# First head of a routed attention kernel: identity in a transfer of its own, first exponential ahead of the next head's copies, codes in another order

## The chip, the cores and the metric

The kernel runs on one core of a Trainium2 chip. A core has five engines with an instruction queue each: PE (TensorE, matrix products; its weight loads are listed as PEld), DVE (VectorE), ACT (ScalarE), POOL (GpSimd) and SP (SyncE, which here only issues transfers). An engine works its queue in order and waits on semaphores that other engines or transfers raise. The metric is the device time of one execution in microseconds (us), the median over several runs.

## The reference

Bucketed attention, then a routed mixture of experts, then a gated product. Only the first part matters here:

```python
q_bits = (np.einsum('bhsd,dk->bhsk', q, proj) > 0)      # 6 bits per query, the same for keys
q_bucket = np.sum(q_bits * powers, axis=-1)
mask = q_bucket[:, :, :, None] == k_bucket[:, :, None, :]
scores = np.where(mask, scale * q @ k^T, -1000000000.0)  # B=2, H=8, S=768, D=64, fp32
attn = exp(scores - max) / (sum + 1e-09)
out = attn @ v
```

A query attends only to the keys of its bucket. The result goes through a router of 8 experts (each token to one of them) and a last product pair; those stages are not touched.

## The kernel before, in words

The 16 pairs of batch and head are called heads 0 to 15. One head has 768 queries, which are 6 tiles of 128; tiles are numbered through all heads by `g`, so head 0 has tiles 0 to 5 and head 1 begins with tile 6.

Inputs of a head come transposed, queries and keys in one buffer `x` (128 partitions, 1536 columns), of which there are two (`xp`, two buffers), so the inputs of head 2 go into the buffer of head 0. For fp32 precision each operand is taken apart: `split_a` (ACT, L105) makes the rounded part `tq` (queries) or `tk` (keys), `split_b` makes the low part `bq` (DVE L117 for the difference, POOL or ACT L118 for a copy) or `bk` (POOL or DVE L120 and L121).

The bucket test is part of the score product. `hash_mm` (PE L130, tile `m`) projects the inputs, and 12 rows of bits, the codes, go into rows 64 to 76 of `tq` and `tk`; with them the product of a query and a key of other buckets comes out far away. For head 0 `hash_code` (DVE L137) writes these rows directly, 384 columns at a time. For all other heads `hash_codes` (DVE L144) writes a tile `code`, and four transfers on SP's queue (L149; two halves of `tq`, then two of `tk`) carry its rows into place. They may start only when the copies that read those rows of `tq` and `tk` are over.

One tile `g` then runs through these steps:

- `scores(g)`: four products on PE (L160 with `tk`, `tq` and the codes; L161 with the low parts), two for each half of the keys, into one of two PSUM buffers `s`
- `smax(g)`: a reduction on DVE (L166, `mm`) and a small operation (L167, `sb`) that gives scale and bias
- `sexp(g)`: the exponential on ACT (L175), into `p`
- `tposes(g)`: six transposes on PE (L188, `tp`) against the identity `ident`, which is the first 128 columns of the constants `cs`; then two copies into `pt` (L192 on ACT, L194 on DVE, by a table)
- later, in the next head, `av_step`: products with V (PE L203)

The order of each engine's queue is that of the code (`tc.manual_schedule()`). In the loop over tiles, the pass of tile `g` first issues `scores(g + 1)` and `smax(g + 1)`, then `set_up(g)` in head 0, then the transposes of tile `g`; `side(pos)` puts exponential, splits and codes before, between or behind the two halves of the transposes, by the table `K`. A few products of a unit matrix (`heat`) run on PE while the first inputs come in. A single element copy `held` on POOL makes POOL wait for the reduction that was issued last.

Of the kernel before, what the change touches and what calls it, by code (L numbers as in the profile page):

```python
# [15 lines left out]
ALU = mybir.AluOpType  # L16
# [5 lines left out]
S, D, NB, NH = 768, 64, 2, 8  # L22
# [12 lines left out]
def attn_moe_kernel(ctx: ExitStack, tc: tile.TileContext, xin, cst, projd, wblk, wmoe, w2in, out):  # L35
    nc = tc.nc
# [69 lines left out]
            T[h, i][:, lo:lo + n], X[h][:, i * S + lo:i * S + lo + n], ACTF.Copy, scale=(-0.125, 1.0)[i]  # L106
        )

    def split_b(h, i, lo=0, n=S):
        copy = POOL.tensor_copy if h or i else ACT.copy  # L110
        x = X[h][:, i * S + lo:i * S + lo + n]
        if lo == 0:
            B[h, i] = tb.tile([128, S], F32R, tag="b" + "qk"[i], name="b" + "qk"[i])
        b = B[h, i][:, lo:lo + n]
        t = T[h, i].bitcast(F32)[:, lo:lo + n]
        if i == 0:
            DVE.scalar_tensor_tensor(out=b[:64], in0=x[:64], scalar=-0.125, in1=t[:64], op0=ALU.mult, op1=ALU.subtract)  # L117
            copy(b[64:], t[64:])  # L118
        else:
            (POOL if h else DVE).tensor_tensor(out=b[64:], in0=x[64:], in1=t[64:], op=ALU.subtract)  # L120
            copy(b[:64], t[:64])  # L121
# [342 lines left out]
    def after(ins, done):  # L464
        ins = ins.ins
        for other in done:
            tc.add_manual_dep(ins, other.name, dep, reason="reads what all the scatters wrote")
# [169 lines left out]
    with tc.manual_schedule():  # L637
# [9 lines left out]
        for j, q in ((2, nc.sync), (3, nc.sync), (0, nc.scalar), (1, nc.sync)):  # L647
            x0_in.append(q.dma_start(out=X[0][:, j * 384:(j + 1) * 384], in_=xin[0, :, j * 384:(j + 1) * 384]).ins)
        nc.scalar.dma_start(out=thr, in_=cst[:, C_THR:C_THR + 2])
        load(1, x0_in)  # L650
        nc.sync.dma_start(out=cs, in_=cst)
        nc.sync.dma_start(out=V[0], in_=xin[0, :, 2 * S:].rearrange("p (k d) -> p k d", d=D))
        nc.sync.dma_start(out=wb, in_=wblk[:, :640 * 2].rearrange("p (h n) -> p h n", h=NH))
        nc.sync.dma_start(out=wl, in_=wblk[:, 640 * 2:])
# [17 lines left out]
        split_a(0, 0, 0, 384)  # L672
        hash_code(0, 2)
        split_b(0, 0, 0, 384)
        hash_code(0, 3)
        hash_code(0, 0)
        scores(0)
        split_a(0, 0, 384, 384)
        split_b(0, 0, 384, 384)
        hash_code(0, 1)  # L680
        smax(0)
        split_a(1, 0)
        split_a(1, 1)
        sexp(0)
        load(2)

        def set_up(k):
            if k == 0:
                split_b(1, 0)
                POOL.tensor_copy(held, pt_[0][:, 0:1])  # L690
            elif k == 1:
                split_b(1, 1)
            elif k == 2:
                POOL.memset(oh, 0.0)
                zero = wraw.tile([128, 512], F32, tag="wr0", name="zero")
                POOL.memset(zero, 0.0)
                zeros.append(zero)
                DVE.tensor_copy(tri, cs[:, C_TRI:C_TRI + 128])
            elif k == 5:
                DVE.tensor_scalar(  # L700
                    out=tokc.bitcast(I32)[:, :, 0], in0=cs[:, C_TOK:C_TOK + 12], scalar1=-float(E * C), scalar2=None,
                    op0=ALU.add,
                )
                DVE.tensor_scalar(
                    out=base2, in0=cs[:, C_BASE:C_BASE + 8], scalar1=1.0 / 128, scalar2=None, op0=ALU.mult
                )
# [32 lines left out]
        qa, qb = (0, 4), (4, 2)  # L739
        for g in range(NG):  # L740
            h, t = divmod(g, NT)
            if t == 1 and h + 3 < NHD:
                load(h + 3)
            if g + 1 < NG:
                scores(g + 1)
                smax(g + 1)
            if g < NT:
                set_up(g)
            if 2 * NT <= g < 2 * NT + (E * C + N) // 256:
                for i in (g - 2 * NT,):  # L750
                    nc.sync.dma_start(
                        out=xr[i * 256:(i + 1) * 256].rearrange("(p r) d -> p r d", p=128),
                        in_=zeros[0].bitcast(U32).unsqueeze(1).to_broadcast([128, 2, 512]),
                    )
            if g == 6 * NT:
                for n in range(4):
                    for part in range(2):
                        w_load(n, part)
            if g == 10 * NT + 1:
                r = router(0)  # L760
                todo = [r["s1"], r["s1b"], None, lambda: (r["s2"](), r["s2c"]()), r["s2b"], r["s4"], r["s4b"]]
                for f in r["sc"]:
                    todo += [f, None]
                todo += [r["s4c"], None, None, None, r["s3a"], None, r["s3b"], None, None, None, r["s5"]]
            early, late = [], []
            if h < L:
                if t == (1 if h else 0):
                    early.append(lambda: hash_mm(h + 1))
                if h:
                    for k in AV_AT.get(t, ()):  # L770
                        early.append(lambda k=k: av_step(h - 1, k))
                if h > 1 and t == 4:
                    (late if K["oul"] else early).append(lambda: o_out(h - 2))
            elif t < 3:
                av_step(h - 1, 2 * t)
                av_step(h - 1, 2 * t + 1)
                if t == 0:
                    o_out(h - 2)
                if t == 2:
                    o_evac(h - 1)  # L780
            elif t == 3:
                o_out(h - 1)
            else:
                k = 3 * (t - 4)
                av_group(h, qa, (k, k + 1, k + 2))
                if t == 5:
                    o_evac(h, qa)
            for f in early:
                f()
            if h and h < L and t == 5 and not K["avl"].count(5):  # L790
                o_evac(h - 1)
            if g > 10 * NT + 1 and todo:
                f = todo.pop(0)
                if f:
                    f()

            def side(pos):
                if g + 1 < NG and K["se" if 0 < h < L else "se0"][t] == pos:
                    sexp(g + 1)
                if h < L and (t, pos) == (1, 0):  # L800
                    hash_codes(h + 1)
                for i in range(2):
                    if h + 2 < NHD and K["sa" if h > 1 else "sa0"][i] == (t, pos):
                        split_a(h + 2, i)
                    if h + 2 < NHD and K["sb" if h > 1 else "sb0"][i] == (t, pos):
                        if t == 5:
                            POOL.tensor_copy(held, last[0])
                        split_b(h + 2, i)

            side(0)  # L810
            tposes(g, 0)
            side(1)
            tposes(g, 1)
            for f in late:
                f()
            if h and h < L and t == 5 and K["avl"].count(5):
                o_evac(h - 1)
            side(2)
            for f in extra.get((h - L + 1, t), ()):
                f()  # L820
        o_out(L, qa)
# [680 lines left out]
```

## Time and profile before

| | |
|---|---|
| median of 3 runs | 722.79 us (722.61 to 722.83) |
| the profiled execution, its own time | 724.47 us |
| its span, first to last instruction | 722.7 us |
| mean granted clock of PE | 0.994 |
| busy: PE, DVE, ACT, POOL | 705.2, 556.8, 448.1, 283.4 us |

The span is what the views of the trace cover; the execution's own time is 1.77 us longer. The profiled execution is one of its own, 1.68 us above the median of the runs without a profile, so a shift is added to either. PE is busy 98% of the span, but matrix products are pipelined and their ends are modelled, so that alone doesn't say that PE sets the pace everywhere. In a row of a timeline the bracket gives the idle time of the engine in front of the instruction and what ended it. PEclk is the clock that PE was granted: 1.00 is 2.4 GHz, 0.50 is 1.2 GHz.

### The profile page before, as it was taken

The numbers are of one execution on the slowest core, as the hardware profiler recorded it, in microseconds if no ns is written. First come the engines' busy times: TensorE is split into PE (matmuls) and PEld (weight loads), VectorE is DVE, ScalarE is ACT, GpSimd is POOL, SyncE is SP. The second block draws the span as 40 slices with busy tenths as digits, with TensorE's granted clock in tenths as the row PEclk, the third lists the DMA queues.
The fourth block names the chain that finished last, engine by engine and source line by source line (L and its number), as shares of the span: only waits on it lengthen the run. The fifth ranks groups of instructions, "written<-read, shape, count | busy, mean of one in ns | idle before, by whom it ended". The sixth has DMA issues, their size and how long they took to land.

```text
span 722.7 us, 13158 instructions
## 1 busy us (share of the span) xinstructions
PE 705.2 (98%) x4505; PEld 604.2 (84%) x4506; DVE 556.8 (77%) x1105; ACT 448.1 (62%) x962; POOL 283.4 (39%) x316
## 2 busy tenths in 40 slices
PE   7899999999999999999999999999999999999995
PEld 6667667667766699999999999999999999999994
DVE  5777887789777778788888878886886877777644
ACT  5787877787877637677778766575444453444320
POOL 4243334322556348845443303333322332223224
PEclk9999999999999999999999999999999999999998
DMA  7348261123212038699899741132121222122013
GB/s 241 107 164 308 85 222 59 59 65 112 104 49 64 15 128 254 174 257 213 237 288 245 229 129 59 40 107 88 59 62 55 88 76 71 55 63 59 0 51 127
DMA packets 53432, 88.01 MB, mean 122 GB/s; under 512 B 19872, under 2 KB 23280, under 8 KB 53360
## 3 DMA queue, kind: packets, MB, share of 16 engines
q1 hardware_dynamic: 50688, 80.61, 37.7%
q0 software_dynamic: 2304, 6.31, 2.3%
q8 instruction: 37, 0.61, 0.3%
q14 instruction: 35, 0.29, 0.1%
q10 hardware_dynamic: 368, 0.20, 0.1%
HBM read 69.65 MB, written 13.12 MB: 115 GB/s over the span
## 4 chain that ended last, share of the span: by engine, by line
PE 84%; issue 4%; DVE 4%; POOL 2%; DMA 2%; ACT 2%; SPq 0%; POOLq 0%; ACTq 0%; DVEq 0%
PE tp L188 9%; PE av L203 8%; PE y L1033 6%; PE s L161 4%; PE s L160 4%; PE h L995 4%; PE h L994 4%; PE h L993 3%; PE aba L1270 3%; PE aba L1272 3%; PE abb L1270 3%; PE aba L1271 3%; PE abb L1272 3%; PE abb L1271 3%; PE y L1034 3%
## 5 line engine op out<-in xcount | busy, mean ns | idle before, releaser
L166 DVE TENSOR_REDUCE mm<-s 128x1 f32<-128x768 f32 x96 | 91.1, 949 | 26.7 <-PE s L161 25.8
L175 ACT ACTIVATE p<-s,sb 128x768 f32<-128x768 f32 x96 | 95.0, 989 | 21.2 <-DVE sb L167 20.4
L188 PEld LDWEIGHTS tp<-cs,p 128*128 128x128 f32 x576 | 64.9, 141 | 37.9 <-ACT p L175 24.4
L188 PE MATMUL tp<-cs,p 128*128 128x128 f32 x576 | 82.7, 280 | 6.4 <-DMA cs<-cst 2.9
L516 DVE TENSOR_TENSOR wl<-wr,wh 128x512 fp32r<-128x512 f32 x125 | 83.2, 705 | 4.9 <-ACT wh L515 1.1
L192 ACT ACTIVATE pt<-tp 128x384 f32<-128x384 f32 x143 | 65.1, 487 | 34.7 <-PE tp L188 34.7
L964 POOL TENSOR_TENSOR pc<-t,pc 128x256 fp32r<-128x256 f32 x38 | 33.1, 873 | 134.8 <-ACT pc L963 119.2
L1033 PE MATMUL y<-hl,wh 128*128 128x448 f32 x224 | 75.0, 378 | 0.6 <-DVE hl L1007 0.5
L515 ACT ACTIVATE wh<-wr 128x512 fp32r<-128x512 f32 x128 | 73.7, 624 | 1.3 <-DMA wr<-wmoe 1.2
L160 PE MATMUL s<-tk,tq 76*128 76x384 f32 x192 | 73.7, 384 | 0.3 <-DVE tq L137 0.3
L994 PE MATMUL h<-xl,wh 128*128 128x224 f32 x256 | 70.3, 275 | 0.5 <-DVE xl L450 0.3
L995 PE MATMUL h<-xh,wl 128*128 128x224 f32 x256 | 70.6, 276 | 0.0
L993 PE MATMUL h<-xh,wh 128*128 128x224 f32 x256 | 70.3, 275 | 0.2 <-ACT xh L449 0.2
L203 PE MATMUL av<-pt,v 128*64 128x384 f32 x360 | 68.0, 499 | 0.2 <-DVE r L238 0.2
L161 PE MATMUL s<-bk,bq 128*128 128x384 f32 x192 | 65.6, 342 | 0.0
L1034 PE MATMUL y<-hl,wl 128*128 128x224 f32 x224 | 59.5, 266 | 0.0
L964 POOL TENSOR_TENSOR pc<-s,pc 128x256 fp32r<-128x256 f32 x44 | 38.0, 875 | 33.0 <-ACT pc L963 32.0
L118 POOL CAST bq<-tq 64x768 fp32r<-64x768 f32 x15 | 21.2, 1414 | 74.8 <-ACT tq L105 47.4
L1160 ACT ACTIVATE gh<-p 128x384 fp32r<-128x384 f32 x21 | 11.0, 526 | 63.2 <-DVE p L1289 63.2
L993 PEld LDWEIGHTS h<-xh,wh 128*128 128x128 f32 x256 | 48.9, 191 | 1.5 <-ACT xh L449 0.4
L994 PEld LDWEIGHTS h<-xl,wh 128*128 128x128 f32 x256 | 49.1, 192 | 1.0 <-DVE xl L450 0.5
L203 PEld LDWEIGHTS av<-pt,v 128*64 128x64 f32 x360 | 21.9, 136 | 32.8 <-issue 24.5
(264 smaller groups left out, 2002.6 us busy)
## 6 DMA issues: line engine op xcount, KB each, us to landing
wr<-wmoe SPq DMA_DIRECT2D x128, 256.0 KB
r<-w2in SPq DMA_DIRECT2D x36, 512.0 KB
x<-xin SPq DMA_DIRECT2D x30, 384.0 KB
xr<-zero SPq DMA_DIRECT2D x13, 512.0 KB
v<-xin SPq DMA_DIRECT2D x16, 192.0 KB
wb<-wblk SPq DMA_DIRECT2D x1, 640.0 KB
x<-xin SPq DMA_DIRECT2D x3, 192.0 KB
tq<-code SPq DMA_DIRECT2D x30, 18.0 KB
```

The costliest lines, as they stand in the source:

```text
L160: PE.matmul(p[:, c, :384], T[h, 0][:76, qs], T[h, 1][:76, sl], start=True, stop=False)
L161: PE.matmul(p[:, c, :384], B[h, 0][:, qs], B[h, 1][:, sl], start=False, stop=True)
L166: DVE.tensor_reduce(out=m[:, 1:2], in_=st[g][:, :, :384], axis=AX.XY, op=ALU.min)
L175: ACT.activation(p.rearrange("p (c n) -> p c n", c=2), st.pop(g)[:, :, :384], ACTF.Exp, scale=scl.pop(g), bias=nbs.pop(g), accum_out=sums[ ...
L188: PE.transpose(ps[:, j * 128:(j + 1) * 128], pt_[g][:, k * 128:(k + 1) * 128], ident)
L203: PE.matmul(av[h][c * 64:(c + 1) * 64, :384], v, PT[h][:, k, c * 384:(c + 1) * 384], start=(k == 0), stop=(k == NT - 1), skip_group_check= ...
L516: eng.tensor_tensor(out=l, in0=r, in1=h.bitcast(F32), op=ALU.subtract)
L993: PE.matmul(ps, wh, xh, start=first, stop=False)
L994: PE.matmul(ps, wh, xl, start=False, stop=False)
L995: PE.matmul(ps, wl, xh, start=False, stop=last)
L1033: PE.matmul(p, wh[:, w], hl, start=(f == 0), stop=False, skip_group_check=True)
L1034: PE.matmul(p[:, 0], wl[:, w], hl[:, 0], start=False, stop=(f == 7), skip_group_check=True)
```

## The change

It touches the first head alone. The identity is transferred by itself when head 0's inputs have landed, ahead of head 1's inputs; the other constants follow where all of them stood. Head 0's codes are written in the order keys' first half, queries' first half, keys' second half; the queries' second half and the low part of that half move behind the reductions of tiles 0 and 1. ACT makes head 1's splits at the ends of tiles 0 and 1, behind the first exponentials, and no longer ahead of them. POOL makes the low part of head 1's keys in two halves, in the passes of tiles 1 and 2, and the low part of head 1's queries follows in the pass of tile 2. The projection of head 1 (`hash_mm(1)`) goes from the pass of tile 0 to that of tile 1, its codes (`hash_codes(1)`) from the pass of tile 1 to that of tile 3, and head 3's inputs (`load(3)`) from tile 1 to tile 4.

```diff
--- before.py
+++ after.py
@@ -106,7 +106,7 @@
             T[h, i][:, lo:lo + n], X[h][:, i * S + lo:i * S + lo + n], ACTF.Copy, scale=(-0.125, 1.0)[i]
         )
 
-    def split_b(h, i, lo=0, n=S):
+    def split_b(h, i, lo=0, n=S, parts=(0, 1)):
         copy = POOL.tensor_copy if h or i else ACT.copy
         x = X[h][:, i * S + lo:i * S + lo + n]
         if lo == 0:
@@ -114,8 +114,12 @@
         b = B[h, i][:, lo:lo + n]
         t = T[h, i].bitcast(F32)[:, lo:lo + n]
         if i == 0:
-            DVE.scalar_tensor_tensor(out=b[:64], in0=x[:64], scalar=-0.125, in1=t[:64], op0=ALU.mult, op1=ALU.subtract)
-            copy(b[64:], t[64:])
+            if 0 in parts:
+                DVE.scalar_tensor_tensor(
+                    out=b[:64], in0=x[:64], scalar=-0.125, in1=t[:64], op0=ALU.mult, op1=ALU.subtract
+                )
+            if 1 in parts:
+                copy(b[64:], t[64:])
         else:
             (POOL if h else DVE).tensor_tensor(out=b[64:], in0=x[64:], in1=t[64:], op=ALU.subtract)
             copy(b[:64], t[:64])
@@ -647,8 +651,9 @@
         for j, q in ((2, nc.sync), (3, nc.sync), (0, nc.scalar), (1, nc.sync)):
             x0_in.append(q.dma_start(out=X[0][:, j * 384:(j + 1) * 384], in_=xin[0, :, j * 384:(j + 1) * 384]).ins)
         nc.scalar.dma_start(out=thr, in_=cst[:, C_THR:C_THR + 2])
+        after(nc.sync.dma_start(out=ident, in_=cst[:, C_ID:C_ID + 128]), x0_in)
         load(1, x0_in)
-        nc.sync.dma_start(out=cs, in_=cst)
+        nc.sync.dma_start(out=cs[:, C_TRI:], in_=cst[:, C_TRI:])
         nc.sync.dma_start(out=V[0], in_=xin[0, :, 2 * S:].rearrange("p (k d) -> p k d", d=D))
         nc.sync.dma_start(out=wb, in_=wblk[:, :640 * 2].rearrange("p (h n) -> p h n", h=NH))
         nc.sync.dma_start(out=wl, in_=wblk[:, 640 * 2:])
@@ -672,25 +677,24 @@
         split_a(0, 0, 0, 384)
         hash_code(0, 2)
         split_b(0, 0, 0, 384)
+        hash_code(0, 0)
         hash_code(0, 3)
-        hash_code(0, 0)
         scores(0)
         split_a(0, 0, 384, 384)
-        split_b(0, 0, 384, 384)
-        hash_code(0, 1)
+        split_b(0, 0, 384, 384, (1,))
         smax(0)
-        split_a(1, 0)
-        split_a(1, 1)
         sexp(0)
         load(2)
 
         def set_up(k):
             if k == 0:
+                split_b(0, 0, 384, 384, (0,))
+                hash_code(0, 1)
+            elif k < 3:
+                POOL.tensor_copy(held, last[0])
+                split_b(1, 1, (k - 1) * 384, 384)
+            if k == 2:
                 split_b(1, 0)
-                POOL.tensor_copy(held, pt_[0][:, 0:1])
-            elif k == 1:
-                split_b(1, 1)
-            elif k == 2:
                 POOL.memset(oh, 0.0)
                 zero = wraw.tile([128, 512], F32, tag="wr0", name="zero")
                 POOL.memset(zero, 0.0)
@@ -739,7 +743,7 @@
         qa, qb = (0, 4), (4, 2)
         for g in range(NG):
             h, t = divmod(g, NT)
-            if t == 1 and h + 3 < NHD:
+            if t == (1 if h else 4) and h + 3 < NHD:
                 load(h + 3)
             if g + 1 < NG:
                 scores(g + 1)
@@ -764,7 +768,7 @@
                 todo += [r["s4c"], None, None, None, r["s3a"], None, r["s3b"], None, None, None, r["s5"]]
             early, late = [], []
             if h < L:
-                if t == (1 if h else 0):
+                if t == 1:
                     early.append(lambda: hash_mm(h + 1))
                 if h:
                     for k in AV_AT.get(t, ()):
@@ -797,7 +801,7 @@
             def side(pos):
                 if g + 1 < NG and K["se" if 0 < h < L else "se0"][t] == pos:
                     sexp(g + 1)
-                if h < L and (t, pos) == (1, 0):
+                if h < L and (t, pos) == ((1, 0) if h else (3, 0)):
                     hash_codes(h + 1)
                 for i in range(2):
                     if h + 2 < NHD and K["sa" if h > 1 else "sa0"][i] == (t, pos):
@@ -816,6 +820,8 @@
             if h and h < L and t == 5 and K["avl"].count(5):
                 o_evac(h - 1)
             side(2)
+            if g < 2:
+                split_a(1, 1 - g)
             for f in extra.get((h - L + 1, t), ()):
                 f()
         o_out(L, qa)
```

Three places show how the order moves; the number in a name tells buffers and tiles apart and is not the same in both kernels. ACT, from the second split of head 0's queries on (`tq`, `tk` of `x_149` are head 1's, `p` is an exponential, `pt` a copy of transposes), before:

```order
L118 CAST bq_247<-tq_244 64x384
L105 ACTIVATE tq_264<-x_149 128x768
L105 ACTIVATE tk_266<-x_149 128x768
L175 ACTIVATE p_268,sums_100<-s_252,sb_261 128x768
L175 ACTIVATE p_293,sums_100<-s_276,sb_281 128x768
L192 ACTIVATE pt_295<-tp_296 128x3x128
L192 ACTIVATE pt_295<-tp_301 128x3x128
L192 ACTIVATE pt_295<-tp_328 128x3x128
L175 ACTIVATE p_333,sums_100<-s_311,sb_316 128x768
```

and now (head 1's inputs are `x_150`):

```order
L122 CAST bq_248<-tq_245 64x384
L179 ACTIVATE p_263,sums_100<-s_253,sb_260 128x768
L179 ACTIVATE p_281,sums_100<-s_271,sb_276 128x768
L196 ACTIVATE pt_283<-tp_284 128x3x128
L196 ACTIVATE pt_283<-tp_289 128x3x128
L105 ACTIVATE tk_294<-x_150 128x768
L196 ACTIVATE pt_283<-tp_313 128x3x128
L179 ACTIVATE p_318,sums_100<-s_296,sb_301 128x768
L105 ACTIVATE tq_325<-x_150 128x768
L196 ACTIVATE pt_283<-tp_345 128x3x128
```

The two splits of head 1 went from ahead of the exponential of tile 0 to behind the copies of tile 0 and behind the exponential of tile 2.

DVE, from head 0's codes to head 1's (each `mm` with its `sb` is one tile's reduction, in the order of tiles; `code` is head 1's), before:

```order
L137 TENSOR_SCALAR tk_236<-m_206,thr_79 12x384
L137 TENSOR_SCALAR tq_244<-m_213,thr_79 12x384
L117 SCALAR_TENSOR_TENSOR bq_247<-x_137,tq_244 64x384
L137 TENSOR_SCALAR tq_244<-m_213,thr_79 12x384
L166 TENSOR_REDUCE mm_101<-s_252 128x1
L167 SCALAR_TENSOR_TENSOR sb_261<-mm_101 128x2
L166 TENSOR_REDUCE mm_101<-s_276 128x1
L167 SCALAR_TENSOR_TENSOR sb_281<-mm_101 128x2
L117 SCALAR_TENSOR_TENSOR bq_284<-x_149,tq_264 64x768
L166 TENSOR_REDUCE mm_101<-s_311 128x1
L167 SCALAR_TENSOR_TENSOR sb_316<-mm_101 128x2
L144 TENSOR_SCALAR code_322<-m_288,thr_79 128x384
```

and now, from the reductions of tiles 0 and 1 (which stand right ahead of this piece) to head 1's codes:

```order
L118 SCALAR_TENSOR_TENSOR bq_248<-x_137,tq_245 64x384
L141 TENSOR_SCALAR tq_245<-m_214,thr_79 12x384
L170 TENSOR_REDUCE mm_101<-s_296 128x1
L171 SCALAR_TENSOR_TENSOR sb_301<-mm_101 128x2
L198 COPY pt_283<-tp_320 128x3x128
L170 TENSOR_REDUCE mm_101<-s_327 128x1
L171 SCALAR_TENSOR_TENSOR sb_332<-mm_101 128x2
L118 SCALAR_TENSOR_TENSOR bq_338<-x_150,tq_325 64x768
L702 CAST tri_83<-cs_75 128x128
L198 COPY pt_283<-tp_350 128x3x128
L170 TENSOR_REDUCE mm_101<-s_359 128x1
L171 SCALAR_TENSOR_TENSOR sb_364<-mm_101 128x2
```

Head 1's `code` is the next instruction behind this piece. It went from behind the reduction of tile 2 to behind that of tile 4; the second half of head 0's queries went behind the reductions of tiles 0 and 1, and head 1's low part of the queries from ahead of the reduction of tile 2 to ahead of that of tile 4.

SP's queue, from head 2's inputs on, before:

```order
L98 DMA x_270<-xin 128x768 x2
L100 DMA v_273<-xin 128x384
L98 DMA x_306<-xin 128x768 x2
L100 DMA v_309<-xin 128x384
L149 DMA tq_264<-code_322 12x384 x2
L149 DMA tk_266<-code_322 12x384 x2
```

and now:

```order
L98 DMA x_265<-xin 128x768 x2
L100 DMA v_268<-xin 128x384
L153 DMA tq_325<-code_367 12x384 x2
L153 DMA tk_294<-code_367 12x384 x2
L98 DMA x_388<-xin 128x768 x2
L100 DMA v_391<-xin 128x384
```

The inputs of head 3 went from ahead of head 1's codes to behind them.

## Rows read from the trace of the kernel before

**Rows 1.** The page: PE's busy tenths in 40 slices, and the chain that ended last.
```profile
PE   7899999999999999999999999999999999999995
...
PE 84%; issue 4%; DVE 4%; POOL 2%; DMA 2%; ACT 2%; SPq 0%; POOLq 0%; ACTq 0%; DVEq 0%
```

**Rows 2.** Timeline of the start (start, us, engine, line, out<-in, count, [idle <-releaser]).
```profile
7.05 1.29 PE L661 MATMUL warm<-ones 128*128 128x128 bf16 x20
...
7.32 0.62 DVE L137 TENSOR_SCALAR tk<-m,thr 12x384 fp32r<-12x384 f32 x1
...
8.64 0.44 PE L160 MATMUL s<-tk,tq 76*128 76x384 f32 x1 [0.30 <-DVE tq L137]
...
9.84 0.96 DVE L166 TENSOR_REDUCE mm<-s 128x1 f32<-128x768 f32 x1
...
10.25 0.85 PE L130 MATMUL m<-x,pst 128*32 128x384 f32 x8
...
11.10 0.99 ACT L175 ACTIVATE p<-s,sb 128x768 f32<-128x768 f32 x1 [0.25 <-DVE sb L167]
...
14.03 0.95 PE L188 MATMUL tp<-cs,p 128*128 128x128 f32 x6 [2.92 <-DMA cs<-cst]
```

**Rows 3.** Windows: length, busy us (count) of PE, PEld, DVE, ACT, POOL; PEclk; DMA.
```profile
14.00:14.50 0.50, 0.47 (x5) 0.50 (x6) 0.00 (x0) 0.00 (x0) 0.50 (x1) 1.00 1.02 409
...
15.00:15.50 0.50, 0.50 (x3) 0.50 (x3) 0.00 (x0) 0.50 (x2) 0.50 (x1) 0.50 1.04 389
...
18.50:19.00 0.50, 0.41 (x4) 0.38 (x4) 0.43 (x2) 0.07 (x1) 0.00 (x0) 1.00 0.98 375
...
20.00:21.00 1.00, 0.26 (x3) 0.05 (x1) 1.00 (x2) 1.00 (x3) 0.00 (x0) 1.00 0.13 34
```

**Rows 4.** Timeline, issues on SP's queue: the constants, the codes of head 1.
```profile
7.26 0.43 SPq L651 DMA_DIRECT2D cs<-cst  x1
...
18.07 1.69 SPq L149 DMA_DIRECT2D tq<-code  x2
...
19.80 1.47 SPq L149 DMA_DIRECT2D tk<-code  x2
```

**Rows 5.** DMA, GB/s in 40 slices of 18 to 24 us.
```profile
GB/s 143 184 205 369 328 379 379 420 328 379 318 205 154 41 31 31 102 41 0 0 0 92 31 0 0 0 92 31 0 0 0 0 0 0 0 0 0 0 0 0
```

**Rows 6.** DMA, GB/s in 40 slices of 0.5 to 6.5 us.
```profile
GB/s 0 0 0 0 0 0 0 0 51 123 113 113 369 389 328 389 349 330 151 82 133 133 154 225 236 328 338 329 247 175 113 53 11 0 0 0 0 0 0 0
```

**Rows 7.** Timeline, small and first transfers and their first readers.
```profile
1.10 0.56 ACTq L645 DMA_DIRECT2D pst<-projd  x1
...
4.00 0.16 DVE L655 COPY pst<-pst 64x6 f32<-64x6 f32 x1 [3.89 <-DMA pst<-projd]
...
5.83 0.52 ACT L105 ACTIVATE tq<-x 128x384 fp32r<-128x384 f32 x1 [0.79 <-DMA x<-xin]
```

**Rows 8.** Timeline of tiles 5 to 7, and a split and a low part.
```profile
20.80 0.83 ACT L105 ACTIVATE tq<-x 128x768 fp32r<-128x768 f32 x1
...
21.67 0.95 DVE L117 SCALAR_TENSOR_TENSOR bq<-x,tq 64x768 fp32r<-64x768 f32 x1 [0.19 <-DMA tk<-code]
...
23.74 0.42 PE L160 MATMUL s<-tk,tq 76*128 76x384 f32 x1
...
24.72 0.96 DVE L166 TENSOR_REDUCE mm<-s 128x1 f32<-128x768 f32 x1
...
25.16 0.88 PE L188 MATMUL tp<-cs,p 128*128 128x128 f32 x6 [0.47 <-ACT p L175]
...
25.74 0.49 ACT L192 ACTIVATE pt<-tp 128x384 f32<-128x384 f32 x1
...
26.13 0.99 ACT L175 ACTIVATE p<-s,sb 128x768 f32<-128x768 f32 x1
...
27.26 0.87 PE L188 MATMUL tp<-cs,p 128*128 128x128 f32 x6 [0.52 <-ACT p L175]
...
30.99 0.88 PE L188 MATMUL tp<-cs,p 128*128 128x128 f32 x6
```

## The prediction

> **What bounds the kernel now.** I read the page first. PE is busy in nine tenths or more of every slice from the third on, and the chain that ended last runs 84% over PE [rows 1]. So whatever moves the first tiles of head 0 is carried to the end almost one for one; the question is only how much earlier or later PE reaches the point where it no longer waits. That point is tile 6: from its transposes on, PE has score products, the codes' products of head 2 and the first products with V to do, and the transposes of tile 7 start 3.73 us behind those of tile 6 (27.26 and 30.99) [rows 8].
>
> Next the timeline of the start. I call s(g) the score products of tile g, mm(g) the row reduction behind them, exp(g) the exponential and tp(g) the six transposes. exp(0) starts at 11.10 and would let tp(0) start about 1.13 us later (exp(6) at 26.13, tp(6) at 27.26 [rows 8]), at 12.2. But tp(0) starts at 14.03, after 2.92 us in which PE stood still for the constants [rows 2], which are issued as one transfer at 7.26, behind head 1's inputs [rows 4]. The windows show a second price: the granted clock, still 1.00 in the first half microsecond after that pause, is 0.50 at 15.0 (the 1.2 GHz level of the two) and 1.00 again at 18.5 [rows 3]. In the stall ACT, POOL and PE did work for head 1 (two splits, the copies, the codes' products), which cost nothing there.
>
> **The change, step by step.** Durations are those of the rows; the sum is made on the profiled execution, 724.47 us with a span of 722.7. The median of the runs, 722.79, is 1.68 below it, and the shift is added to both alike.
>
> Identity first. It is 64 KB, issued when head 0's inputs have landed (ACT reads them at 5.83 [rows 7]), and not at 7.26. No row shows it landing alone. From below: a transfer of 1.5 KB was read 2.34 us after its issue ended (1.66, 4.00); from above: a quarter of head 0's inputs, issued behind that on the same queue, was read at 5.83, 4.2 us on [rows 7]. So the identity is there between 8.7 and 10.4, before any tile wants it, and at either bound it costs nothing.
>
> Tile 0. The codes change places, so the last one that s(0) needs is over after two of 0.62 us from 7.32, at 8.6. PE is busy with its warm-up products to 8.34, so s(0) starts then instead of at 8.64, and mm(0), which stood behind another code and a split to 9.84, can start at 9.35 [rows 2]. From a reduction to its exponential it is 1.26 us (9.84, 11.10), so exp(0) starts at 10.6 and tp(0) at 11.7: **2.3 us earlier than 14.03**.
>
> Tiles 1 to 4. Here the work that lay in the stall comes back. PE: tp(0) takes 0.7 before the next product can start, s(2) 0.8, the codes' products 0.85 [rows 2], so tp(1) starts at 14.0. ACT: the copy of tile 1 starts 0.58 behind that and exp(2) 0.39 later (25.16, 25.74, 26.13 [rows 8]), at 15.0; tp(2) at 16.1. Behind exp(2) stands the query split of head 1 (0.83 [rows 8]), over at 16.8, then a copy, then exp(3) at 17.1; tp(3) at 18.2. DVE: the low part of that split (0.95 [rows 8]) waits in front of mm(4) and runs from 16.8 to 17.8; with the cast of the constants and one copy, some 0.8 together by the 0.49 of a copy on ACT, mm(4) starts at 18.6, though s(4) would let it start at 17.8. exp(4) at 19.85, tp(4) at 21.0. By that count s(6) could start at 21.7, 2.0 ahead of 23.74.
>
> Codes of head 1. They now stand behind mm(4), not behind mm(2). The code runs from 19.7 to 20.4, and s(6) needs it in the rows of head 1's transposed inputs, to which four transfers carry it. Before, the first was issued at 18.07 and the last issue ended at 21.27 [rows 4]; the last traffic of the four lies in slices 27 and 28 of 0.15 us, to 22.20 [rows 5]. So from code to last byte 4.15 us. From the last byte to a reader's start: head 0's inputs end in slice 33, by 5.45, and ACT reads at 5.83 [rows 6, 7], about 0.4. The last code is thus there at 20.4 + 4.15 + 0.4 = 25.0. Only the second half of s(6) wants it, and that half starts 0.44 behind the first (0.42 for its first product [rows 8]), so s(6) starts in effect at 24.55: **0.8 us later than 23.74, where it could be 2.0 earlier**. Bounds: the last byte alone gives 24.1; the 2.34 us of the small transfer after its issue [rows 7] give 20.4 + 3.2 + 2.34 - 0.44 = 25.5. I take 24.55, since the traffic of these very transfers shows it. The Trainium skill, DMA: Bandwidth & Descriptors, section Anatomy of one DMA, gives each transfer a fixed part of about 2.0 us, most of it the receipt of the write; by that, an estimate, s(6) starts at 25.2 and the sum is 0.6 longer.
>
> Behind s(6) on PE stand tp(5) and all else. mm(6) starts 0.98 behind s(6) (23.74, 24.72), exp(6) 1.23 later, tp(6) 1.13 later: 27.9, against 27.26. Laid by the same steps, the order of before comes to 27.66, 0.40 above its row, so the shift is between +0.25 and +0.64; I take +0.45. From the idle time of PE in front of s(6), below, +0.15 on average. Sum **+0.6 us**: 724.47 + 0.6 for a profiled execution, 722.79 + 0.6 = **723.4 us** for the median.
>
> Edits that cost nothing here. Head 1's inputs come one issue (0.43 us [rows 4]) later; their first reader is now ACT at 13.4, the cover is some 3 us, and without it each 0.1 us late is 0.1 us lost. Head 2's inputs wait for the later split of head 0, but the DMA engines are full to 15.5 anyway (1.04 in the window from 15.0 [rows 3]) and ACT wants them at 18.0. Head 3's inputs go behind the codes on SP's queue, at about 23.6, and are wanted in tile 8, ten microseconds on. POOL has its copies of head 1 in two halves behind reductions 2 and 3; they end by 20, just ahead of the codes that must not overwrite what POOL reads; if POOL is later than 20.4, the codes and s(6) are later by as much.
>
> **The rivals.** *The codes are not waited for.* Then tp(5) is held by exp(5) alone, tp(6) starts at 25.85 and the gain is 1.4 to 1.8: 721.2 us. It needs s(6) at 22.4 or earlier, so codes that land within 2.5 us of their start on SP; the four issues alone took 3.2 [rows 4]. For it speaks only that DVE may reach the code earlier than I lay it, which has to be by 1.5 us or more. Chance 0.18; it decides from a code that is over by 18.9.
>
> *The clock falls in the first pause.* PE stands still from 9.95 (s(1) done, codes' products moved away) to 11.7, 1.75 us, and again for some 2.3 in front of s(6). A pause of 2.92 was followed by half clock [rows 2, 3]; a window with only 0.26 of 1.00 us busy kept 1.00 [rows 3]. Half clock from tile 0 on stretches tp(0), s(2), the codes' products and tp(1) by some 1.4 us altogether, with nothing else beside them to hide it, and all later steps move with them: 0.45 + 1.4 = 1.85, 724.7 us. In front of s(6) the same fall costs only about 0.3, because the exponentials set the pace of the next two tiles; at an even chance that is the 0.15 in the sum. The Trainium skill, TensorE: Matmul & The Clock Gate, Part 1, calls the low clock the default that activity lifts; by that rule each longer pause of the new order is at risk. Chance 0.15.
>
> *The codes land by the upper bound*, s(6) at 25.5: +1.4, with a fall of the clock behind it +1.7: 724.3. Chance of ending beyond +1.45: 0.10.
>
> **How the numbers follow.** About 0.2%, or 1.45 us, is what a measurement of this kernel can tell from no change. The forecast, a gain in tile 0 that is used up by tile 6, holds 0.57 and lies within that; its own range is 722.2 to 724.2. Faster 0.18 is the first rival, slower 0.25 the other two. The range of 721.0 to 724.8 takes in the first rival's time and the second's, and leaves out about 0.15.
>
> **What would show it.** Right: tp(0) near 11.7 without a wait for the constants; full clock to about 21; then a wait of PE in front of s(6) of some 2 us whose releaser is the transfers of codes; tp(6) within half a microsecond of 27.9. Wrong: s(6) without a wait near 22; or 0.50 of clock in a window between 12 and 16. The steps most likely to fail are the place of the code on DVE's clock and the time from code to reader.

## The result, and the profile after

The changed kernel takes **729.35 us** (median of 4 runs, 729.15 to 729.86), the kernel before 722.81 (4 runs beside them, 722.61 to 722.93). The ratio is 1.0092, 95% interval 1.0074 to 1.0109: slower by 6.5 us, where a time of 723.4 was predicted. The profiled execution took 729.15 us with a span of 727.4 and a mean granted clock of 0.989 (before: 724.47, 722.7, 0.994).

The page of the changed kernel, PE's busy tenths and the chain that ended last, as in [rows 1]:

```profile
PE   8799999999999999999999999999999999999995
...
PE 82%; POOL 7%; issue 5%; DVE 3%; ACT 1%; DMA 1%; POOLq 0%; SPq 0%; DVEq 0%; ACTq 0%
```

POOL's share has gone from 2% to 7%. PE's timeline of the changed kernel, tiles 0 to 7, beside [rows 2, 8] (line numbers are 4 or 5 higher; the row of PEld is the weight load of the second half of s(6)):

```profile
12.20 1.49 PE L192 MATMUL tp<-cs,p 128*128 128x128 f32 x6 [1.72 <-ACT p L179]
...
14.90 1.23 PE L134 MATMUL m<-x,pst 128*32 128x384 f32 x8
...
16.06 0.88 PE L192 MATMUL tp<-cs,p 128*128 128x128 f32 x6
...
22.75 0.93 PE L192 MATMUL tp<-cs,p 128*128 128x128 f32 x6 [0.89 <-ACT p L179]
...
26.25 0.66 PE L164 MATMUL s<-tk,tq 76*128 76x384 f32 x1 [2.57 <-DMA tk<-code]
...
26.94 0.29 PEld L164 LDWEIGHTS s<-tk,tq 76*128 76x128 f32 x1 [0.22 <-DMA tk<-code]
...
27.74 1.48 PE L192 MATMUL tp<-cs,p 128*128 128x128 f32 x6
...
30.43 1.54 PE L192 MATMUL tp<-cs,p 128*128 128x128 f32 x6
...
35.26 0.88 PE L192 MATMUL tp<-cs,p 128*128 128x128 f32 x6
```

tp(0) no longer waits for constants and starts 1.83 us earlier than in [rows 2]. But it takes 1.49 instead of 0.95, and tp(1) comes only at 16.06. Before s(6) PE stands 2.57 us, released by the codes' transfers; the second half of s(6) waits for them once more. tp(7) is 4.27 us later than 30.99 in [rows 8].

Windows of the changed kernel, beside [rows 3] (length, busy us and count of PE, PEld, DVE, ACT, POOL; granted clock; DMA):

```profile
12.50:15.50 3.00, 3.00 (x14) 2.17 (x16) 1.10 (x2) 2.31 (x5) 0.00 (x0) 0.50 0.93 319
...
24.00:26.00 2.00, 0.00 (x0) 0.00 (x0) 0.68 (x3) 1.65 (x3) 0.10 (x1) 0.99 0.10 23
26.00:32.00 6.00, 5.75 (x21) 5.03 (x22) 3.09 (x7) 2.22 (x5) 2.52 (x3) 0.50 0.49 167
```

Two stretches stand at 0.50, the 1.2 GHz level: 12.5 to 15.5, behind the pause of 1.72 us, and 26 to 32, behind the pause in front of s(6). The rows of DVE, POOL and SP that lead to the codes (for the issues, beside [rows 4]):

```profile
18.98 0.90 POOL L694 COPY held<-sb 128x1 f32<-128x1 f32 x1 [0.91 <-DVE sb L171]
...
21.44 0.67 DVE L148 TENSOR_SCALAR code<-m,thr 128x384 fp32r<-128x384 f32 x1
21.56 0.82 POOL L122 CAST bq<-tq 64x768 fp32r<-64x768 f32 x1
22.03 1.16 DVE L118 SCALAR_TENSOR_TENSOR bq<-x,tq 64x768 fp32r<-64x768 f32 x1
22.41 1.69 SPq L153 DMA_DIRECT2D tq<-code  x2
...
24.15 1.47 SPq L153 DMA_DIRECT2D tk<-code  x2
...
24.91 0.71 SPq L153 DMA_DIRECT2D tk<-code  x1
```

The code is over at 22.11, POOL's last copy of rows that the codes overwrite at 22.38, and SP issues at 22.41: POOL ends last. (The last row is the second of the two transfers of the row above it.) Before, the issue was at 18.07 [rows 4].

### The profile page after: what moved, and what is told of

Same layout as the page of the kernel before. It is cut to its first block, busy times and chain, and to the rows that moved or that the text cites. A ratio compares the mean times of both kernels' runs of the same rounds, so it can differ in the third digit from the quotient of the medians.

```text
span 727.4 us, 13160 instructions
## 1 busy us (share of the span) xinstructions
PE 709.0 (97%) x4505; PEld 606.9 (83%) x4506; DVE 556.5 (77%) x1105; ACT 447.4 (62%) x962; POOL 283.9 (39%) x319
## 4 chain that ended last, share of the span: by engine, by line
PE 82%; POOL 7%; issue 5%; DVE 3%; ACT 1%; DMA 1%; POOLq 0%; SPq 0%; DVEq 0%; ACTq 0%
PE tp L192 9%; PE av L207 8%; PE y L1039 5%; PE s L164 4%; PE s L165 4%; PE aba L1276 3%; PE aba L1278 3%; PE aba L1277 3%; PE abb L1276 3%; PE abb L1278 3%; PE abb L1277 3%; PE h L1001 3%; PE h L999 3%; PE h L1000 3%; PE q L1206 3%
## 5 line engine op out<-in xcount | busy, mean ns | idle before, releaser
L1001 PEld LDWEIGHTS h<-xh,wl 128*128 128x128 f32 x256 | 49.2, 192 | 0.0
```

Source lines behind the costliest of these rows:

```text
L1001: PE.matmul(ps, wl, xh, start=False, stop=last)
```

## The experiments

Theory A: the loss is the wait for head 1's codes in front of s(6), and the half clock after PE's pauses. Theory B: the copies and reductions of head 1, moved out of the stall into the tiles, make DVE and POOL late by themselves. The first execution of before that was profiled may also be no typical one, so before was profiled again. Where an expectation gives its theories a meaning for its own run, that one holds there.

The table holds, of each profiled execution, the start of the first score product, tp(6) and their distance (an execution starts its products at 7.9 to 9.5, so distances compare better than times), and of the timed runs the ratio to before, its interval and the number of runs.

| kernel | first s | tp(6) | distance | ratio | interval, runs |
|---|---|---|---|---|---|
| before, of the rows above | 8.64 | 27.26 | 18.62 | 1 | |
| before again (e8) | 9.47 | 25.49 | 16.02 | 1 | |
| the change | 8.67 | 30.43 | 21.76 | 1.0092 | 1.0074 to 1.0109, 4 |
| e1 identity alone | 9.23 | 25.26 | 16.03 | 1.0003 | 0.9988 to 1.0018, 12 |
| e2 POOL and codes early | 8.65 | 29.05 | 20.40 | 1.0059 | 1.0039 to 1.0079, 6 |
| e3 fill in the first pause | 9.07 | 29.29 | 20.22 | 1.0061 | 1.0042 to 1.0079, 6 |
| e4 fill in both pauses | 8.93 | 28.73 | 19.80 | 1.0051 | 1.0033 to 1.0069, 6 |
| e5 e2 and fill in the first | 8.04 | 27.34 | 19.30 | 1.0062 | 1.0049 to 1.0075, 6 |
| e6 codes early | 7.92 | 28.27 | 20.35 | 1.0052 | 1.0034 to 1.0069, 4 |
| e7 POOL early | 9.21 | 31.39 | 22.18 | 1.0123 | 1.0108 to 1.0138, 4 |
| e9 e2 and fill in both | 9.06 | 30.00 | 20.94 | 1.0088 | 1.0075 to 1.0101, 5 |
| e10 identity, code order | 9.28 | 27.74 | 18.46 | 1.0025 | 1.0014 to 1.0035, 12 |
| e11 e10, exponential first | 8.35 | 25.98 | 17.63 | 1.0036 | 1.0023 to 1.0049, 5 |
| e12 the change, no codes | 8.08 | 25.62 | 17.54 | 1.0028 | 1.0015 to 1.0040, 12 |
| e13 e12 and fill in the first | 8.55 | 25.92 | 17.37 | 1.0038 | 1.0026 to 1.0051, 7 |
| e14 e10, low part first | 8.43 | 26.46 | 18.03 | 1.0045 | 1.0028 to 1.0063, 10 |

**Before once more (e8), and the identity alone (e1).** e8 is before without an edit, 722.15 us in its one execution. e1 is before with two lines of the change:

```diff
+        after(nc.sync.dma_start(out=ident, in_=cst[:, C_ID:C_ID + 128]), x0_in)
         load(1, x0_in)
-        nc.sync.dma_start(out=cs, in_=cst)
+        nc.sync.dma_start(out=cs[:, C_TRI:], in_=cst[:, C_TRI:])
```

> The kernel before once more, for a second profile of it. Theory A (the clock's rise and fall at the start differ from one execution to the next, and the gain of the identity alone shows only against an execution with the fall): a start of the codes' products other than 5.18, no half clock between 14.5 and 18, and a span of 720 to 721.5. Rival B: the same stretch of half clock as in the first profile and a span of 722.5 or more.

> The kernel before with one part of the change alone: the identity in a transfer of its own ahead of head 1's inputs. Theory A (the loss of the whole change is made at s(6): codes that come late because POOL's copies stand behind reductions, and PE at half clock after its pauses): tp(0) near 12.3 without a wait for the constants, PE idle only some 1.1 us there since the codes' products of head 1 still fill it, full clock throughout, and 720.5 to 721.8 us. Rival B (the identity displaces head 1's inputs, and their later splits are the price): first split of head 1 waits to 9.5 or later, the exponential of tile 0 is later by as much, and the time is 722.6 or more.

ACT, DVE and PE of e8 in its timeline:

```profile
11.93 0.99 ACT L175 ACTIVATE p<-s,sb 128x768 f32<-128x768 f32 x1 [1.01 <-DVE sb L167]
...
12.81 0.95 DVE L117 SCALAR_TENSOR_TENSOR bq<-x,tq 64x768 fp32r<-64x768 f32 x1
...
13.06 0.88 PE L188 MATMUL tp<-cs,p 128*128 128x128 f32 x6 [1.13 <-ACT p L175]
```

and one of its windows:

```profile
14.00:18.00 4.00, 3.12 (x22) 2.56 (x21) 3.24 (x7) 2.80 (x7) 3.26 (x4) 1.00 0.80 284
```

Here tp(0) waits for the exponential and not for the constants, the granted clock stays at 1.00 behind it, and the pause is 1.13 us. So the 2.92 us and the half clock of [rows 2, 3] are not in each execution of the kernel, and the timed runs say that they are in few: of the 68 runs of before beside these experiments, four have a mean granted clock of 0.994, as the first profiled execution had, and they took 724.20 to 725.53 us; the others have 0.995 to 0.999. (A mean clock doesn't show where it fell.) The identity alone gains nothing that 12 runs can tell: e1 measures 723.08 beside 723.43, against 720.5 to 721.8 by theory A. Nor do head 1's displaced inputs cost anything, as its rival B has it: exp(0) starts 2.46 us behind the first score product in both, and the distance is that of e8.

**Fill products (e3, e4).** Unit products keep PE at work in the pauses: 20 ahead of tp(0) in e3, and in e4 24 more ahead of s(6) (the first part of the diff is e4's alone).

```diff
+            if g == 5:
+                fill = ps_a.tile([128, 512], F32, tag="a", name="fill")
+                for i in range(24):
+                    PE.matmul(fill[:, :128], ones, ones, start=True, stop=True)
             if g + 1 < NG:
                 scores(g + 1)
...
+            if g == 0:
+                heat(20)
             side(0)
```

> The changed kernel, with 20 products of a unit matrix on PE in the first pause, between s(1) and tp(0); nothing reads them. Theory A: the granted clock stays at 1.00 through tiles 0 and 1, tp(1) starts near 14.6 in place of 16.06, POOL and the codes follow, s(6) near 24.8, and the time is 727.0 to 728.0 us. Rival B (half clock in tiles 0 and 1 is hidden by ACT's splits): tp(1) earlier, s(6) and the time as in the changed kernel, 729.0 to 729.8.

> As the kernel with products in the first pause, and 24 more of them in front of s(6). Theory A: the second stretch of half clock (26.0 to 32.7 in the changed kernel) is gone as well, which is worth 1.5 to 2.5 us more: 724.8 to 726.3. Rival B (the second stretch costs 0.3, since the exponentials set the pace there): within 0.5 of the kernel with products in the first pause alone.

e3: 727.89 us, e4: 726.95. PE's rows of e3 for s(6), tp(6) and tp(7):

```profile
25.11 0.66 PE L164 MATMUL s<-tk,tq 76*128 76x384 f32 x1 [2.57 <-DMA tk<-code]
...
29.29 1.35 PE L192 MATMUL tp<-cs,p 128*128 128x128 f32 x6
...
33.50 0.88 PE L192 MATMUL tp<-cs,p 128*128 128x128 f32 x6
```

In e4 the clock is 1.00 throughout, and the wait is still there. Its timeline, and two windows:

```profile
21.11 1.69 SPq L153 DMA_DIRECT2D tq<-code  x2
...
24.94 0.41 PE L164 MATMUL s<-tk,tq 76*128 76x384 f32 x1 [1.23 <-DMA tk<-code]
...
28.73 0.87 PE L192 MATMUL tp<-cs,p 128*128 128x128 f32 x6 [1.13 <-ACT p L179]
...
32.47 0.87 PE L192 MATMUL tp<-cs,p 128*128 128x128 f32 x6
```

```profile
22.00:25.00 3.00, 1.77 (x28) 1.62 (x27) 1.38 (x3) 2.30 (x4) 0.80 (x1) 1.00 0.10 21
25.00:32.00 7.00, 5.78 (x38) 3.74 (x40) 4.71 (x10) 3.72 (x8) 2.81 (x3) 1.00 0.42 145
```

The 1.23 us come behind 1.50 us of fill. From the change's ratio to e4's it is 0.41%, some 3.0 us, for the two falls of the clock. The first is the larger: 0.31% or 2.2 us from the change to e3, and in the rows 1.54 at tp(6) (21.76 to 20.22) and 0.62 to tp(7) (4.83 to 4.21). From e3 to e4 it is 0.10% or 0.7 us, which the intervals don't tell from nothing, and in the rows 0.42 and 0.47 (4.21 to 3.74). That lies between e4's two theories, 1.5 to 2.5 us and 0.3. About half of the loss is none of the clock's.

**Where the codes are held (e2, e5, e6, e7, e9).** In e6 the code moves from the pass of tile 3 to that of tile 2. In e7 it stays, and POOL makes head 1's low parts whole, a pass earlier, without `held`. e2 does both, e5 adds the 20 products of e3, e9 also the 24 of e4. The first part of the diff is in e2, e5, e6 and e9, the second in e2, e5, e7 and e9.

```diff
-                if h < L and (t, pos) == ((1, 0) if h else (3, 0)):
+                if h < L and (t, pos) == ((1, 0) if h else (2, 0)):
...
-                POOL.tensor_copy(held, last[0])
-                split_b(1, 1, (k - 1) * 384, 384)
+                split_b(1, 2 - k)
             if k == 2:
-                split_b(1, 0)
```

> The changed kernel, with POOL's copies of head 1 no longer behind reductions 2 and 3 (whole, in the passes of tiles 1 and 2, without the held copies) and head 1's codes in the pass of tile 2 in place of 3. Theory A: the four transfers are issued at 20.5 to 20.8 in place of 22.41, s(6) starts at 24.4 to 24.8 in place of 26.25, and the time is 726.0 to 727.6 us. Rival B (the price is ACT's splits and the codes' products inside the tiles): s(6) earlier, but the time stays within 0.7 of 729.35.

> The changed kernel with head 1's codes in the pass of tile 2 in place of 3, POOL as in the change. Theory A (the transfers wait for POOL's last copy, at 22.38, not for the code on DVE): they are issued at 22.0 to 22.5 although the code is over by 20.6, and the time stays within 0.9 of 729.35 us. Rival B (the code's place on DVE decides, as the prediction had it): issue at 20.6 to 21.2 and 1.2 to 1.8 us less.

> The changed kernel with POOL's copies early, the codes still in the pass of tile 3. Theory A: POOL is done by 20.6, and the transfers then wait for the code on DVE, so they are issued near 22.0, 0.3 to 0.5 sooner than in the changed kernel: 728.3 to 729.3 us. Rival B (POOL alone was in the way): issue near 21.2 and a time as with both parts early, 727.3.

> Both repairs at once in the changed kernel: POOL's copies and the codes early, and 20 products of a unit matrix in the first pause. Theory A (late codes and half clock are two causes, the second feeding the first): s(6) starts between 23.3 and 24.0, no stretch of half clock, and the time is 724.0 to 725.5 us, still above the kernel before by the splits, products and copies that lay in its stall. Rival B (either repair alone already gives what there is): 726.7 to 727.5, as with one of them.

> The change with POOL's copies and the codes a pass earlier and 20 unit products in the first pause, as in the run before, and now 24 unit products ahead of s(6) as well. Theory A: the loss is the wait for the codes plus half clock, nothing else; with full clock throughout and the codes there at about 23, tp(6) comes at 26 or before and the time is within 1 us of before. Theory B: what is left is DVE, where the low part of the queries, the cast of the constants and the code stand ahead of a copy and of mm(4), work that lay in the stall before; tp(4) is still near 22 against 21.3, tp(6) near 26.7, and the time stays 1.2 to 2.5 us above before, the clock notwithstanding.

Measured: e2 727.32 us, e6 725.37, e7 731.14, e5 726.81, e9 728.92. In e6 POOL alone holds the codes; DVE is done at 18.39:

```profile
17.73 0.66 DVE L148 TENSOR_SCALAR code<-m,thr 128x384 fp32r<-128x384 f32 x1
...
19.40 0.83 POOL L122 CAST bq<-tq 64x768 fp32r<-64x768 f32 x1
20.25 1.69 SPq L153 DMA_DIRECT2D tq<-code  x2
...
24.08 0.66 PE L164 MATMUL s<-tk,tq 76*128 76x384 f32 x1 [1.07 <-DMA tk<-code]
```

In e7 POOL is done at 21.02, but DVE's code then ends only at 23.37 and the issue follows at 23.43: either engine alone can hold it. Issues at 19.38 to 21.2 (e2, e5, e6) give back 2 to 3 us, and not the whole loss. Of the expectations only e2's theory A and e5's rival B meet the measured time; e6 is below both of its theories, e7 and e9 above both of theirs. ACT and PE of e5:

```profile
20.93 0.99 ACT L179 ACTIVATE p<-s,sb 128x768 f32<-128x768 f32 x1 [1.53 <-DVE sb L171]
...
22.06 1.54 PE L192 MATMUL tp<-cs,p 128*128 128x128 f32 x6 [0.83 <-ACT p L179]
...
23.26 0.67 PE L164 MATMUL s<-tk,tq 76*128 76x384 f32 x1
```

In e5 the wait in front of s(6) is gone, and most of the loss is not. Two things took its place: exp(4) waits 1.53 us for DVE (1.46 in e2, 1.54 in e9, 0.27 in the change), where the code now stands ahead of mm(4) and the cast of the constants takes 0.84 beside POOL's cast (0.21 in the change), and the clock fell ahead of tp(4) and stood at 0.50 from 21 to 27. e9 was meant to leave only theory B and did not: the clock fell ahead of its fill, the 24 products took 2.77 us instead of 1.50, and s(6) stood behind them until 26.42. By its time it tells nothing of A against B, only that a fill at half clock can cost what it should save.

**The wait taken away (e12, e13).** The four transfers of head 1's codes are left out, so head 1 tests its buckets with other rows, and the router gets other values for head 1; all else is made. e13 adds the 20 products of e3.

```diff
-        for j in range(4):
+        for j in range(0 if h == 1 else 4):
```

> The change without the four transfers that carry head 1's codes (head 1 then tests its buckets with wrong rows; all products, reductions and copies are made). Theory A (the loss is the wait for these transfers in front of s(6), about 3.2 us in tiles 5 and 6, with the half clock that follows that pause, about 1.6 us, and the half clock after the first pause, 1.5 to 2.4 us): s(6) starts behind tp(4) without a wait, tp(6) about 27, and the time is 3.4 to 4.8 us below the change. Theory B (the steps of tiles 1 to 5 are late by DVE's and POOL's work in them, and the wait only uses up time that is lost anyway): within 1.5 us of the change.

> The run above with 20 unit products in the first pause too, so that neither the codes nor the first fall of the clock is left. Theory A: level with before, within 1 us. Theory B: 2 us or more above before.

e12: 725.01 us, e13: 725.36. ACT, DVE and PE in the timeline of e13:

```profile
19.95 0.99 ACT L179 ACTIVATE p<-s,sb 128x768 f32<-128x768 f32 x1 [0.28 <-DVE sb L171]
...
20.36 1.16 DVE L118 SCALAR_TENSOR_TENSOR bq<-x,tq 64x768 fp32r<-64x768 f32 x1
...
21.08 0.93 PE L192 MATMUL tp<-cs,p 128*128 128x128 f32 x6 [0.92 <-ACT p L179]
...
22.68 0.99 ACT L179 ACTIVATE p<-s,sb 128x768 f32<-128x768 f32 x1 [0.52 <-DVE sb L171]
...
23.82 0.88 PE L192 MATMUL tp<-cs,p 128*128 128x128 f32 x6 [1.08 <-ACT p L179]
...
25.92 0.87 PE L192 MATMUL tp<-cs,p 128*128 128x128 f32 x6 [0.52 <-ACT p L179]
```

Without the wait 0.64% of 0.92% is back in e12, 4.6 us, the half clock behind the wait included: theory A's mechanism, shown. But e13 is not below e12, so the fill that is worth 2.2 us in e3 is worth nothing here; the profiled execution of e12 had no fall in the first pause, and whether its timed runs had isn't known. What is left in both is slower than before by 0.3 to 0.4%, so theory A's "level with before" falls for e13, and B's "2 us or more" holds. The trace has part of it: exp(4) and exp(5) now wait for DVE, whose low parts and code stand ahead of mm(4) and mm(5), and tp(6) is 1.35 us later after the first score product than in e8 (17.37 against 16.02). The rest isn't placed: the stages after attention, from the last product with V to the last product of all, take 2.6 us longer in e12, 2.3 in e13 and 0.9 in the first execution of before than in e8, and single traces don't tell whether an edit, or head 1's other values, have to do with it.

**The early parts by themselves (e10, e11, e14).** e10 is e1 with head 0's codes in the change's order, head 1's work where it was before. e11 puts `sexp(0)` ahead of head 1's splits in it; e14 puts `split_b(1, 0)` first in `set_up(0)`.

```diff
             if k == 0:
+                split_b(0, 0, 384, 384, (0,))
+                hash_code(0, 1)
                 split_b(1, 0)
```

> Before with two parts of the change alone: the identity's transfer, and head 0's codes in the new order with the queries' second half behind the reductions of tiles 0 and 1. Head 1's splits, copies, projection and codes stay where they were. Theory A (the loss comes only from head 1's work, moved out of the stall): mm(0) starts some 1.2 us earlier, exp(0) follows head 1's splits on ACT at once, tp(0) 0.8 to 1.0 us earlier than with the identity alone, and every later tile too: 0.5 to 1.0 us faster than before. Theory B (the early start itself is lost, in the pace of 2.1 us per tile or in a clock that falls): the same as before within 0.4 us, or slower.

> The run above and the first exponential ahead of head 1's two splits on ACT, which then stand between the first exponential and the second. Theory A: tp(0) is earlier by another 0.4 us or so, but exp(1) waits for 1.7 us of splits, so tp(1) and all later tiles come some 1 us later than in the run above, and head 1's codes too; slower than the run above by 0.7 to 1.5 us. Theory B (the exponential's place is the gain of the change): as fast as the run above or faster.

> Before with the identity's transfer and head 0's codes in the new order, as in a run above, but head 1's low part of the queries on DVE directly behind the reduction of tile 1, ahead of head 0's second half of the queries. Theory A (in the run above this instruction took 2.10 us for 0.95 because POOL was at its own difference at the time, and that made mm(2) late by 1.1 us): it takes 0.95 again, mm(2) starts about 1 us earlier, and the time is 1.0 to 1.6 us below that run's 1.0025 of before: 0.9990 to 1.0005. Theory B (that run lost by the clock after the early start): still 1.002 or more.

Measured: e10 724.09 us, e11 724.91, e14 724.99 (before 722.44 beside the first two, 722.84 beside the third). None gains; three of e14's ten runs took 728.4 to 728.6, the others 724.2 to 725.5. In e10 DVE and POOL hold each other up:

```profile
13.27 1.82 POOL L124 TENSOR_TENSOR bk<-x,tk 64x768 fp32r<-64x768 f32 x1
13.80 2.10 DVE L118 SCALAR_TENSOR_TENSOR bq<-x,tq 64x768 fp32r<-64x768 f32 x1
15.15 1.44 POOL L125 CAST bk<-tk 64x768 fp32r<-64x768 f32 x1
```

and the clock fell, as its theory B names; one of its windows:

```profile
21.00:23.00 2.00, 2.00 (x9) 1.86 (x8) 1.04 (x2) 1.77 (x5) 1.54 (x1) 0.50 0.15 47
```

DVE's difference and POOL's cast take 0.95 and 0.82 in e8, where DVE's came first. e14 has DVE's back at 0.95 and mm(2) 1.6 us earlier (0.7 counted from the first score product, where about 1 was expected), and its clock is 1.00 from 9 to 36, but the time is no better: its price in the expectation was wrong. By its rows the time went to the inputs of head 2, which can come only when head 0's buffer has been read; with that reader moved, they are issued at 13.80 instead of 10.07 in e8, run into head 3's, and the codes land behind both. SP and PE of e14:

```profile
13.80 0.80 SPq L98 DMA_DIRECT2D x<-xin  x2
...
15.38 0.80 SPq L98 DMA_DIRECT2D x<-xin  x2
...
18.50 1.47 SPq L153 DMA_DIRECT2D tk<-code  x2
...
23.08 0.41 PE L164 MATMUL s<-tk,tq 76*128 76x384 f32 x1 [1.22 <-DMA tk<-code]
```

From the last issue's end (19.97) to s(6) it is 3.11 us there, where the change takes 1.32 (25.62 to 26.94). That the inputs cause it is read from these rows; no run took them away. e11's exponential does not gain over e10, but the two intervals meet, so the price of the splits behind it stays open.

## Why the prediction was wrong

723.4 was predicted for the median and 729.35 measured. Three steps failed: the base to which the sum was added (1.66 us), the fall of the clock in the first pause, which was priced as a rival and left out of the sum (1.5 us at s(6)), and the price of the fall behind s(6) (0.15 in the sum, 1.5 in the rows). The wait for the codes itself was sized rightly.

**Identity, tile 0.** Right as a mechanism: tp(0) at 12.20 without a wait for constants, and at 11.79 in e12, for 11.7. But the 2.3 us credited for it were the gain over an execution that is not typical. In e8 tp(0) doesn't wait for constants, and e1 gains nothing. The failed step is that "the shift is added to both alike": the profiled execution lay 1.68 us above the median with the very stall and half clock that the change was to remove, and a typical execution has none of it to give. Of the 6.54 us in the medians, 1.66 are this (724.47 against 722.81). e12 shows it from the other side: its tp(6) at 25.62 is that of the first rival (25.85), for which 721.2 us were predicted, and it takes 725.01.

**Tiles 1 to 4.** In e12, an execution without a fall of the clock in these tiles, tp(1) to tp(4) start at 14.09, 16.19, 18.29 and 20.79, for 14.0, 16.1, 18.2 and 21.0. So the steps were right, and what the sum left out was the clock. In the change's profile it fell in the first pause, as the second rival had it at a chance of 0.15: tp(1) is 7.39 behind the first score product, against 5.85 in e3 (14.92), so 1.54 later, for the 1.4 of that rival.

**Codes of head 1.** The wait was at the place that was named. From SP's first issue to the second half of s(6) it took 4.53 us (22.41 to 26.94), for 4.55. The issue, though, came at 22.41 and not at 20.4, by the clock: counted from the first score product it is 13.74 in the change, 12.18 in e4 without the first fall, and 12.06 in the prediction (20.4 and 8.34). So with s(6): 17.58 in the change, 16.04 in e3, and 16.21 in the prediction. POOL's copies, which were to "end by 20", end at 22.38, and in e12 at 20.42. The condition that "if POOL is later than 20.4, the codes and s(6) are later by as much" is what happened.

**The second fall.** "In front of s(6) the same fall costs only about 0.3" was wrong. Half clock lasted from 26.0 to 32.8; from s(6) to tp(6) it is 4.18 us, for 3.34 by the predicted steps (0.98, 1.23 and 1.13), and from tp(6) to tp(7) 4.83 for 3.73: together 1.9 us. Not all of it is the clock's, since e4 at full clock takes 3.79 and 3.74: the clock's part is 1.5 us, and about 0.9 in e3, where half clock ended 5.2 us behind the start of s(6) and not 6.5. The exponentials don't set the pace there, since tile 6 has nearly four microseconds of products behind it, as the prediction's own first part says.

**The sum.** Of the 5.95 us between the forecast and the median, 1.66 are the base, 1.70 a later s(6) (26.25 for 24.55) and 1.94 what came behind it to tp(7). The rest is small, and part of it can't be checked: the 27.66 for the order of before "by the same steps" is not worked out in the prediction; from s(6) at 23.74 its steps give 27.08. In the profiled executions s(6) is 2.51 us later than before, and with 1.76 more behind it tp(7) is 4.27 later. Against e8, counted from the first score product, the change is 5.74 later at tp(6), and 1.1 more at tp(7): 6.84, near the 6.54 of the medians, and 6.86 at attention's last product with V. e4 and e13 divide it: 1.96 and the 1.1 for the clock (21.76 to 19.80), 2.43 for the wait (19.80 to 17.37), 1.35 for DVE's and POOL's work in the tiles (17.37 to 16.02). The timed ratios give 3.0, 0.9 and 2.7 us for the three, with e12 in e13's place 1.7 and 2.0 for the last two, and each ratio's interval reaches about 1 us to either side: the clock's share is the same by both, that of the wait against the rest is not settled.

## What to carry to other kernels

Before a stall is priced, profile the unchanged kernel a second time: here the stall and the half clock that the change aimed at were in one execution and missing in the next. Work that lies in a stall is free there only, so count every instruction that must leave it, the other engine's copies that release its transfers too, and what its own move delays (a buffer that comes free later, a pause that opens elsewhere). A pause in front of dense products costs its own length and, in some executions, half clock behind it.

## What the runs showed of the hardware

- **The clock after a pause** is not the same in each execution. A pause of 1.72 us ahead of tp(0) was followed by some 3 us at 0.50 in the change, in e2 and in e7, and by 1.00 in e6 (to 20) and in e12 (to 36). In e6 it fell in a pause of 1.30 us ahead of tp(4), by 21.0, and was at 0.50 to 27.5.
- **DVE and POOL.** DVE's difference of two inputs took 0.95 alone, 1.16 beside a cast on POOL, and 2.10 beside POOL's difference. POOL's copy of one element, `held`, took 0.18 to 0.90. The Trainium skill, SBUF — State Buffer, section SBUF: two separate sides, has the two engines share a port pair as an exclusive lock when DVE reads two SBUF inputs and POOL reads SBUF; e10's rows agree: DVE's 2.10 is close to its own 0.95 and the 1.29 that POOL's 1.82 still had to run at 13.80.
- **Small transfers** of the codes: in the change the last of the four was read 2.03 us after its issue began (24.91 to 26.94) and 1.32 us after it ended, with the DMA engines 10% busy; in e14, where the inputs of two heads were on the way, 3.11 us after the end. The Trainium skill, DMA: Bandwidth & Descriptors, section Anatomy of one DMA, gives a fixed part of about 2.0 us to a transfer that is issued on GpSimd's queue; these were issued on SP, and from the start of the issue their 2.03 us are close to it. The prediction, which set it beside its own term, counted it from the end of the last issue.
